# Widening the stationary of the last 64-token tiles from 64 to 128 columns

## The chip, the cores and the metric

The kernel runs on one core of a Trainium2 chip. The metric is the device time of one execution in microseconds (us). Engines are named as the profile does: PE is TensorE's matmuls, PEld its weight loads, DVE is VectorE, ACT is ScalarE, POOL is GpSimd.

## The reference, cut to what matters

Linear attention with a feature map, followed by a two-layer feed-forward block:

```python
# q, k, v: [8 batches, 8 heads, 576 tokens, 64];  w_phi: [64, 128]
def phi(x):                                   # 64 -> 128 -> 256 features
    proj = einsum('bhsd,df->bhsf', x, w_phi)
    proj = proj - max(abs(proj), axis=-1)
    return concatenate([exp(proj), exp(-proj)], axis=-1)
kv  = einsum('bhsf,bhsd->bhfd', phi(k), v)
z   = sum(phi(k), over tokens)
num = einsum('bhsf,bhfd->bhsd', phi(q), kv)
den = einsum('bhsf,bhf->bhs', phi(q), z) + 1e-6
x   = (num / den) as [4608 tokens, 512]
out = relu(x @ w_in)**2 @ w_out               # 512 -> 2048 -> 512
```

Per batch, 576 tokens are four tiles of 128 tokens and one of 64. The change concerns the product that gives num and den for that last tile.

## The kernel before

A list scheduler in Python orders all work in one program. It interleaves the attention of batch b with the feed-forward matmuls (128x512, the bulk of the work) of earlier tokens. Three kinds of TensorE matmul matter. The profile writes the stationary as rows\*columns, "128\*64" being 128 rows by 64 columns:

- feed-forward: 128\*128, mostly 512 moving columns;
- projections of q and k, and the kv product: 64\*128, issued in pairs on rows 0 to 63 and 64 to 127 of their operands (called row-tiled here; in the trace the second of such a pair mostly starts 3 or 4 ns after the first);
- num/den: the stationary is exp(±proj) of one head for the tile's tokens, the moving operand is kv with 65 columns. For a 128-token tile that is 128\*128, for the 64-token tile 128\*64 (called column-tiled here).

The forms that are neither, 128\*128, are called the full array. A switch of mode is a change from one of these three kinds to another. The words sort the forms that the profile lists; what TensorE does at a switch no trace shows, only when things start.

```python
for i, (g0, j0, nj) in enumerate(order_j):          # nj = 2: 128 tokens; nj = 1: 64 tokens
    lo, hi_ = g0 % 2 * 64, (g0 % 2 + nj) * 64       # the tile's rows: 0:128, 0:64 or 64:128
    ...
    # exponentials of the projections, two banks bk, two signs, into qph (t), packed
    nc.scalar.activation(
        out=t.t.rearrange("f pr hi p -> f (pr hi p)")[:, : nj * 512].rearrange(
            "f (r b c) -> f b r c", r=2, b=2)[:, bk],
        in_=w[bk].t[:, : nj * 256].rearrange("f (r c) -> f r c", r=2),
        func=ACT.Exp, scale=sg)
    ...
    for r in range(2):                              # two groups of four heads, a PSUM bank each
        def nd(c, w=w, lo=lo, hi_=hi_):
            return w.t.rearrange("t (h c) -> t h c", h=4)[lo:hi_, :, c]
        def fn(s, ...):                             # s: the sign; four matmuls, one per head
            for z in range(4):
                h = 4 * r + z
                nc.tensor.matmul(
                    out=nd(slice(0, D + 1))[:, z],
                    lhsT=qg[s].t.rearrange("f pr hi p -> f (pr hi p)")[
                        :, h * (hi_ - lo) : (h + 1) * (hi_ - lo)],
                    rhs=kv[r][0].t[:, z % 2, z // 2, s, :],
                    start=(s == 0 and z == 0), stop=True, skip_group_check=True)
        # PE: fn(0); DVE: scale by em; PE: fn(1); DVE: reciprocal of den, then num * that -> xo
    # xo is transposed into xT by DMA (batch 0: by PE); the feed-forward matmuls read xT
```

The eight 64-token tiles issue 8 x 2 x 2 groups of 4, so 128 column-tiled matmuls, out of 4194.

Of the kernel before, what the change touches and what calls it, by code (L numbers as in the profile page):

```python
# [157 lines left out]
def kernel(  # L158
# [12 lines left out]
    B, H, S, D = q.shape  # L171
    Fd = w_phi.shape[1]
    DM, DF = moe_w_in.shape
    P = 128
# [56 lines left out]
    def pe(key, cost, fn, deps=(), bufs=(), rows=128):  # L231
        o = pl.op("pe", cost, key, fn, deps, bufs, lat=350, rows=rows)
        att.append(o)
        return o

    def act(key, n, fn, deps=(), bufs=()):
        return pl.op("act", 60 + 0.83 * n, key, fn, deps, bufs, lat=220 + MARGIN)

    def dve(key, n, fn, deps=(), bufs=()):

        return pl.op("dve", 65 + 1.04 * n, key, fn, deps, bufs, lat=190 + MARGIN)
# [6 lines left out]
    def banks(n):  # L248

        w = [Buf(r_one) for _ in range(n)]  # L250
        for x in w:
            x.token = Buf(r_att)
        return w
# [25 lines left out]
    def begin():  # L279
# [5 lines left out]
        out=scrap[:, 4:8], in_=scrap[:, 0:4], func=ACT.Exp), [o_begin])  # L285
# [56 lines left out]
    def attention(b, x, key):  # L342
# [4 lines left out]
        def transposes(xb, ld, xt, at):  # L347

            ops = []
            if b >= NPE or b and at:  # L350
                for u0, n in GRP:
                    def fn(u0=u0, n=n):
                        nc.sync.dma_start_transpose(
                            out=xt.t[:, u0 // 2 : (u0 + n) // 2, :],
                            in_=xb.t[:, u0 : u0 + n, :].rearrange("x u d -> x (u d)"),
                        )
                    ops.append(xbar(key(at), n * 16, fn, ld[0] + (x["v"][1][0] if b > 1 else []), [xb, xt]))
                return ops
            for u0, n in ((0, 16), (16, 16), (32, 4)) if b or at else GRP:
                w, = banks(1)  # L360

                def fn(u0=u0, n=n, w=w):
                    for i in range(n // 2):
                        nc.tensor.transpose(
                            out=tp(w)[:, i], in_=xb.t[:, u0 + 2 * i : u0 + 2 * i + 2, :]
                            .rearrange("x u d -> x (u d)"), identity=ident)
                kk = key(1 + u0 + 4 * at)
                p_ = pe(kk, 40 + n * 30, fn,
                        [o_id] + ld[0] + (ld[-1] if u0 + n > U // 2 else []), [w, xb, xt])
                ms = slice(u0 // 2, (u0 + n) // 2)  # L370
                if b or at:
                    o = dve(kk, n * 38, lambda w=w, n=n, ms=ms: nc.vector.tensor_copy(
                        out=xt.t[:, ms, :], in_=tp(w)[:, : n // 2]), [p_], [w, xt])
                else:
                    o = act(kk, n * 64, lambda w=w, n=n, ms=ms: nc.scalar.activation(
                        out=xt.t[:, ms, :], in_=tp(w)[:, : n // 2], func=ACT.Copy),
                        [p_], [w, xt])
                ops += [o] * (1 if not (b or at) else (n + 7) // 8)
# [5 lines left out]
        if b:  # L384
            d = pl.op("x", 1000, key(2), None, tq)
            gates[b] = pool(key(2), 100, lambda: nc.gpsimd.tensor_copy(
                out=gate, in_=qT.t[:1, M - 1, P - 8 :]), [d], [qT])
# [4 lines left out]
        if b:  # L392
            def fn():
                nc.gpsimd.memset(va[0].t[:, :, D], 1.0)
                nc.gpsimd.tensor_copy(out=va[0].t[:, :, :D], in_=xv.t)
            o_va = [[pool(key(32), 2400, fn, lv[0] + lv[-1], va[:1] + [xv])] * NG] * 2
# [4 lines left out]
        for g, (u0, n) in enumerate(GRP):  # L401
            kk = key(2 + 8 * g)
            w = banks(2)
            c = n * 64
# [71 lines left out]
        while g0 < (b + 1) * NJ:  # L476
            j0 = jord[b % 2][g0 - b * NJ]
            nj = 1 if j0 == NJ - 1 else 2
# [4 lines left out]
        for hf in range(2):  # L483
            t = Buf(r_kv)
            w = banks(2)

            def kvp(w, hi):
                return w[hi].t.rearrange("f (i c) -> f i c", i=4)[:, :, : D + 1]
            ops = []
            for prl in range(2):  # L490
                pr = 2 * hf + prl
# [18 lines left out]
            for hi in range(2):  # L510
                kk = key(KV_AT[1] + 8 * hf + 6 if b else 20)
                if b or hi:
                    o.append(act(kk, 260, lambda w=w, t=t, hi=hi: nc.scalar.activation(
                        out=t.t[:, hi].rearrange("f pr s c -> f (pr s) c"),
                        in_=kvp(w, hi), func=ACT.Copy), ops, w + [t]))
                else:
                    o.append(dve(kk, 260, lambda w=w, t=t, hi=hi: nc.vector.tensor_copy(
                        out=t.t[:, hi].rearrange("f pr s c -> f (pr s) c"),
                        in_=kvp(w, hi)), ops, w + [t]))
# [5 lines left out]
        for i, (g0, j0, nj) in enumerate(order_j):  # L525
            lo, hi_ = g0 % 2 * 64, (g0 % 2 + nj) * 64
            kk = key(Q2_AT[b > 0][i])
            w, qg = banks(2), [Buf(r_qph), Buf(r_qph)]
# [15 lines left out]
            qe = []  # L544
            for bk in range(2):
                for t, sg in zip(qg, (1.0, -1.0)):
                    def fn(w=w, t=t, sg=sg, nj=nj, bk=bk):
                        nc.scalar.activation(  # L548
                            out=t.t.rearrange("f pr hi p -> f (pr hi p)")[:, : nj * 512].rearrange(
                                "f (r b c) -> f b r c", r=2, b=2)[:, bk],  # L550
                            in_=w[bk].t[:, : nj * 256].rearrange("f (r c) -> f r c", r=2),
                            func=ACT.Exp, scale=sg)
                    qe.append(act(kk, nj * 256, fn, [p_], [w[bk], t]))

# [2 lines left out]
            w, m0, mq, em = banks(2), Buf(r_m0), Buf(r_mq), Buf(r_em)  # L557

            def fn(w=w, j0=j0, nj=nj):
# [12 lines left out]
                out=m0.t[:, bk, : 2 * nj],  # L572
                in_=w[bk].t[:, : nj * 256].rearrange("x (i f) -> x i f", f=Fd),
# [23 lines left out]
            c, tt = tile_of[n2]  # L597
# [8 lines left out]
            for r in range(2):  # L606
                w, = banks(1)
                hs = slice(4 * r, 4 * r + 4)

                def nd(c, w=w, lo=lo, hi_=hi_):  # L610
                    return w.t.rearrange("t (h c) -> t h c", h=4)[lo:hi_, :, c]

                def fn(s, nd=nd, qg=qg, lo=lo, hi_=hi_, r=r):
                    for z in range(4):
                        h = 4 * r + z
                        nc.tensor.matmul(  # L616
                            out=nd(slice(0, D + 1))[:, z],
                            lhsT=qg[s].t.rearrange("f pr hi p -> f (pr hi p)")[
                                :, h * (hi_ - lo) : (h + 1) * (hi_ - lo)],
                            rhs=kv[r][0].t[:, z % 2, z // 2, s, :],  # L620
                            start=(s == 0 and z == 0), stop=True, skip_group_check=True)
                bs = [w, rd, xo, kv[r][0]]
                p_ = pe(kk, 132, lambda fn=fn: fn(0), [o_em] + qe + kv[r][1], bs + [qg[0]])

                def sc(nd=nd, em=em, lo=lo, hi_=hi_, hs=hs):
                    x = nd(slice(0, D + 1))
                    nc.vector.tensor_tensor(  # L627
                        out=x, in0=x, in1=em.t[lo:hi_, hs].to_broadcast(list(x.shape)),
                        op=ALU.mult)
                dk = kk - 20  # L630
                d_ = dve(dk, 260, sc, [p_, o_em], [w, em])
                p_ = pe(dk, 132, lambda fn=fn: fn(1), [d_], bs + [qg[1]])
                d_ = dve(dk, 50, lambda nd=nd, rd=rd, lo=lo, hi_=hi_, hs=hs:
                    nc.vector.reciprocal(out=rd.t[lo:hi_, hs], in_=nd(D)), [p_], [w, rd])

                def fn(nd=nd, rd=rd, xo=xo, lo=lo, hi_=hi_, hs=hs):
                    x = nd(slice(0, D))
                    nc.vector.tensor_tensor(  # L638
                        out=xo.t[lo:hi_].rearrange("t (h d) -> t h d", h=H)[:, hs],
                        in0=x, in1=rd.t[lo:hi_, hs].to_broadcast(list(x.shape)), op=ALU.mult)  # L640
                parts.append(dve(dk, 250, fn, [d_], [w, rd, xo]))
            nds.append(p_)
            if hi_ == P and b == 0:
                w, = banks(1)
# [159 lines left out]
```

## Time and profile before

| | before |
|---|---|
| median of 3 runs (range) | 383.3 us (382.87 to 383.75) |
| span of the profiled execution | 382.5 us |
| PE busy | 366.7 us, 96% |
| DVE / ACT / POOL busy | 65% / 64% / 49% |

Lines of the page of the kernel before: the span, the busy time of the engines, and the chain of work that ended last, by engine and by line. L708 and L679 are the two feed-forward products, L616 is num/den, L500 is the kv product. Of the names in these lines, win and wout are w_in and w_out, qph and kph are phi(q) and phi(k), mk and ksh are the largest absolute value of a k projection and the projection less it, va is v with an added column that gives z, xo is num / den and xT its transpose, hr is the relu and h its square; "one" is any PSUM bank, PSUM being the memory that TensorE writes to.

```profile
span 382.5 us, 10585 instructions
...
PE 366.7 (96%) x4194; PEld 200.9 (53%) x4194; DVE 247.7 (65%) x554; ACT 244.4 (64%) x485; POOL 185.9 (49%) x317
...
PE 74%; DMA 11%; DVE 9%; issue 3%; POOL 1%; DVEq 0%; POOLq 0%
```

PE is three quarters of the chain. The DMA part is loading in the first 49 us (of w_out 8%, of v 2%), and the DVE part is a few stretches in which PE waits for VectorE. A busy share alone would not say that a saved nanosecond counts; the chain says that it does, outside those stretches. (The durations do not give the cost of a matmul: in this trace a 128x512 matmul is recorded with 380 ns, yet the next starts 216 ns after it. So all costs below are read from starts, not from durations.)

Groups by form of the kernel before (line, engine, operation, operands, stationary, shapes, count; busy us, mean ns of one; idle before):

```profile
L616 PE MATMUL one<-kv_sb,qph 128*128 128x65 bf16 x512 | 28.5, 195 | 1.5 <-DVE one L627 1.4
L616 PE MATMUL one<-kv_sb,qph 128*64 128x65 bf16 x128 | 9.1, 200 | 0.0
...
L616 PEld LDWEIGHTS <-qph 128*128 128x128 bf16 x512 | 23.6, 98 | 13.6 <-issue 2.9
L616 PEld LDWEIGHTS <-qph 128*64 128x64 bf16 x128 | 6.1, 110 | 8.6 <-issue 8.5
```

The mean durations of the two forms hardly differ (195 and 200 ns). What the 128\*64 form costs is seen in when things start.

Over the whole trace, matmul by matmul: 309 ns from a 512-column matmul into a 128\*64 run (otherwise 216), and 128 ns out of it (otherwise 30).

### The profile page before, as it was taken

The numbers are of one execution on the slowest core, as the hardware profiler recorded it, in microseconds if no ns is written. First come the engines' busy times: TensorE is split into PE (matmuls) and PEld (weight loads), VectorE is DVE, ScalarE is ACT, GpSimd is POOL, SyncE is SP. The second block draws the span as 40 slices with busy tenths as digits, with TensorE's granted clock in tenths as the row PEclk, the third lists the DMA queues.
The fourth block names the chain that finished last, engine by engine and source line by source line (L and its number), as shares of the span: only waits on it lengthen the run. The fifth ranks groups of instructions, "written<-read, shape, count | busy, mean of one in ns | idle before, by whom it ended". The sixth has DMA issues, their size and how long they took to land.

```text
span 382.5 us, 10585 instructions
## 1 busy us (share of the span) xinstructions
PE 366.7 (96%) x4194; PEld 200.9 (53%) x4194; DVE 247.7 (65%) x554; ACT 244.4 (64%) x485; POOL 185.9 (49%) x317
## 2 busy tenths in 40 slices
PE   8989999978999999999999999999999999999994
PEld 8868857544544454545543544455446444444442
DVE  1857894899279738973699488956895843333221
ACT  3785788649972986489758974996399733333300
POOL 8533766507890986079728674677446420000000
PEclk9998999999999999999999999999999999999998
DMA  7999994257944595459665946495631422112123
GB/s 114 213 208 205 162 174 73 48 91 133 195 50 89 91 217 62 80 105 202 99 85 109 169 85 104 91 196 102 105 77 30 71 55 49 35 29 55 27 64 75
DMA packets 70721, 40.41 MB, mean 106 GB/s; under 512 B 51088, under 2 KB 65552, under 8 KB 70672
## 3 DMA queue, kind: packets, MB, share of 16 engines
q1 hardware_dynamic: 55360, 21.38, 31.2%
q0 software_dynamic: 15312, 18.35, 29.4%
q8 instruction: 33, 0.54, 0.6%
q14 instruction: 16, 0.13, 0.1%
HBM read 36.77 MB, written 9.44 MB: 121 GB/s over the span
## 4 chain that ended last, share of the span: by engine, by line
PE 74%; DMA 11%; DVE 9%; issue 3%; POOL 1%; DVEq 0%; POOLq 0%
PE one L708 32%; PE one L679 25%; DMA wout<-in_moe_w_out_dram 8%; PE one L616 5%; PE one L500 5%; DVE mk L423 4%; DVE ksh L433 3%; PE one L538 3%; DMA xv<-in_v_dram 2%; PE one L567 2%; PE one L412 2%; DVE ot L715 1%; DVE xo L638 1%; POOL va L467 1%; DVE one L627 1%
## 5 line engine op out<-in xcount | busy, mean ns | idle before, releaser
L687 POOL TENSOR_TENSOR h<-hr 128x512 bf16<-128x512 bf16 x112 | 115.2, 1042 | 83.7 <-ACT hr L684 81.7
L679 PE MATMUL one<-xT,win 128*128 128x512 bf16 (+2 forms) x704 | 144.2, 341 | 2.8 <-DVE ksh L433 2.8
L708 PE MATMUL one<-wout,h 128*128 128x512 bf16 x576 | 144.5, 380 | 0.8 <-DMA wout<-in_moe_w_out_dram 0.5
L684 ACT ACTIVATE hr<-one 128x512 bf16<-128x512 f32 x144 | 84.5, 603 | 67.7 <-PE one L679 59.8
L548 ACT ACTIVATE qph<-one 128x512 bf16<-128x512 f32 (+1 forms) x160 | 77.9, 563 | 19.5 <-PE one L538 19.3
L679 PEld LDWEIGHTS <-win 128*128 128x128 bf16 x704 | 59.2, 98 | 54.6 <-issue 3.5
L708 PEld LDWEIGHTS <-h 128*128 128x128 bf16 x576 | 51.0, 98 | 56.6 <-issue 1.4
L441 ACT ACTIVATE kph<-ksh 128x1024 bf16<-128x1024 f32 (+1 forms) x70 | 64.8, 964 | 19.7 <-DVE ksh L433 19.2
L571 DVE TENSOR_REDUCE m<-one 128x4 f32<-128x512 f32 (+1 forms) x80 | 47.9, 630 | 41.7 <-PE one L567 24.9
L423 DVE TENSOR_REDUCE mk<-one 128x4 f32<-128x512 f32 (+1 forms) x80 | 49.7, 627 | 8.3 <-PE one L412 8.2
L433 DVE TENSOR_TENSOR ksh<-one,mk 128x512 f32<-128x512 f32 (+1 forms) x70 | 44.7, 638 | 3.8
L715 DVE COPY ot<-one 128x512 f32<-128x512 f32 x36 | 24.7, 685 | 28.2 <-PE one L708 28.0
L580 POOL COPY mq<-m 64x4 f32<-64x4 f32 x144 | 26.5, 184 | 32.0 <-DVE m L571 27.3
L616 PEld LDWEIGHTS <-qph 128*128 128x128 bf16 (+1 forms) x640 | 29.7, 100 | 22.2 <-issue 11.3
L616 PE MATMUL one<-kv_sb,qph 128*128 128x65 bf16 (+1 forms) x640 | 36.9, 196 | 1.5 <-DVE one L627 1.4
L627 DVE TENSOR_TENSOR one<-one,em 128x260 f32<-128x260 f32 (+1 forms) x80 | 31.5, 429 | 5.8 <-PE one L616 2.3
L638 DVE TENSOR_TENSOR xo<-one,rden 128x256 bf16<-128x256 f32 (+1 forms) x80 | 31.7, 419 | 0.8
L690 DVE TENSOR_TENSOR h<-hr 128x512 bf16<-128x512 bf16 x32 | 13.5, 423 | 24.4 <-ACT hr L684 24.4
L323 PE MATMUL one<-ones 128*128 128x128 bf16 x316 | 24.0, 236 | 1.1 <-DVE scrap L281 1.1
L500 PE MATMUL one<-va,kph 64*128 64x65 bf16 x1152 | 22.8, 191 | 0.9 <-issue 0.9
L500 PEld LDWEIGHTS <-kph 64*128 64x128 bf16 x1152 | 20.5, 94 | 4.3 <-issue 3.3
L323 PEld LDWEIGHTS <-ones 128*128 128x128 bf16 x316 | 20.6, 106 | 2.5 <-DVE scrap L281 1.1
(43 smaller groups left out, 184.5 us busy)
## 6 DMA issues: line engine op xcount, KB each, us to landing
out_dram<-ot SPq DMA_DIRECT2D x72, 128.0 KB, 2.4
xk<-in_k_dram POOLq DMA_DIRECT2D x7, 576.0 KB, 6.1
xq<-in_q_dram POOLq DMA_DIRECT2D x7, 576.0 KB, 9.8
xv<-in_v_dram POOLq DMA_DIRECT2D x7, 576.0 KB, 12.2
win<-in_moe_w_in_dram POOLq DMA_DIRECT2D x1, 2048.0 KB, 18.5
wout<-in_moe_w_out_dram POOLq DMA_DIRECT2D x1, 2048.0 KB, 32.4
xk<-in_k_dram POOLq DMA_DIRECT2D x2, 288.0 KB, 5.6
xq<-in_q_dram POOLq DMA_DIRECT2D x2, 288.0 KB, 7.6
```

The lines of the kernel that those rows point to most:

```text
L323: nc.tensor.matmul(out=r_one.tiles[7][:, :P], lhsT=ones, rhs=ones, start=True, stop=True)
L423: nc.vector.tensor_reduce(out=mk.t[:, e, ms], in_=wv(e), axis=AX.X, op=ALU.max, apply_absolute_value=True)
L433: nc.vector.tensor_tensor(out=ksh.t[:, e, : n // 2, :], in0=wv(e), in1=mk.t[:, e, ms].to_broadcast([P, n // 2, Fd]), op=ALU.subtract)
L441: nc.scalar.activation(out=t.t[:, :, : n // 2, :].rearrange("x e i f -> x e (i f)"), in_=ksh.t[:, :, : n // 2, :].rearrange("x e i f -> x ...
L500: nc.tensor.matmul(out=kvp(w, hi)[:, 2 * prl + s], lhsT=kph[g][s].t[r, i % 2, i // 2, :], rhs=va[s].t[r, u, : D + 1], start=(j == 0), stop ...
L548: nc.scalar.activation(out=t.t.rearrange("f pr hi p -> f (pr hi p)")[:, : nj * 512].rearrange("f (r b c) -> f b r c", r=2, b=2)[:, bk], in ...
L571: d1 = [dve(kk, nj * 256, lambda w=w, m0=m0, nj=nj, bk=bk: nc.vector.tensor_reduce(out=m0.t[:, bk, : 2 * nj], in_=w[bk].t[:, : nj * 256].r ...
L616: nc.tensor.matmul(out=nd(slice(0, D + 1))[:, z], lhsT=qg[s].t.rearrange("f pr hi p -> f (pr hi p)")[:, h * (hi_ - lo) : (h + 1) * (hi_ - ...
L679: nc.tensor.matmul(out=w.t[:, y * n : (y + 1) * n], lhsT=win[:, kc, mc * P : (mc + 1) * P], rhs=xT.t[:, a:z, kc, :], start=(kc == 0), stop ...
L684: o = act(key - 4, TCH, lambda: nc.scalar.activation(out=r.t, in_=w.t, func=ACT.Relu), [p_], [w, r])
L687: o = pool(key - 4, 1050, lambda: nc.gpsimd.tensor_tensor(out=t.t, in0=r.t, in1=r.t, op=ALU.mult), [o], [r, t])
L708: nc.tensor.matmul(out=w.t, lhsT=h2[c, mc, tt][0].t[:, h2[c, mc, tt][1] :][:, :P], rhs=wout[:, mc, :], start=(mc == 0), stop=(mc == KC2 - 1))
```

## The change

The intent: give the 64-token tile a 128-column stationary too, so that no matmul has the column-tiled form. The exponentials of the 64 tokens are written into their half (lo:hi_) of a full 128-wide slot; the other half keeps what an earlier tile left there. The product then gives 128 rows, of which 64 are garbage that nobody reads. Core of the diff:

```diff
-    out=t.t.rearrange("f pr hi p -> f (pr hi p)")[:, : nj * 512].rearrange(
-        "f (r b c) -> f b r c", r=2, b=2)[:, bk],
-    in_=w[bk].t[:, : nj * 256].rearrange("f (r c) -> f r c", r=2),
+    out=t.t.rearrange("f (r b) hi p -> f b r hi p", b=2)[:, bk, :, :, lo:hi_],
+    in_=w[bk].t[:, : nj * 256].rearrange(
+        "f (r hi c) -> f r hi c", r=2, hi=2),
...
-    out=nd(slice(0, D + 1))[:, z],
-    lhsT=qg[s].t.rearrange("f pr hi p -> f (pr hi p)")[
-        :, h * (hi_ - lo) : (h + 1) * (hi_ - lo)],
+    out=w.t[:, z * P : z * P + D + 1],
+    lhsT=qg[s].t[:, h // 2, h % 2, :],
```

The order of instructions on every engine stays the same.

More of the change, by code (lines that the diff above doesn't have):

```diff
@@ L546, in attention, with fn @@
                 for t, sg in zip(qg, (1.0, -1.0)):
-                    def fn(w=w, t=t, sg=sg, nj=nj, bk=bk):
+                    def fn(w=w, t=t, sg=sg, nj=nj, bk=bk, lo=lo, hi_=hi_):
                         nc.scalar.activation(
-                            out=t.t.rearrange("f pr hi p -> f (pr hi p)")[:, : nj * 512].rearrange(
-                                "f (r b c) -> f b r c", r=2, b=2)[:, bk],
-                            in_=w[bk].t[:, : nj * 256].rearrange("f (r c) -> f r c", r=2),
+                            out=t.t.rearrange("f (r b) hi p -> f b r hi p", b=2)[:, bk, :, :, lo:hi_],
+                            in_=w[bk].t[:, : nj * 256].rearrange(
+                                "f (r hi c) -> f r hi c", r=2, hi=2),
                             func=ACT.Exp, scale=sg)
@@ L611, in nd, with fn @@
                     return w.t.rearrange("t (h c) -> t h c", h=4)[lo:hi_, :, c]
-                def fn(s, nd=nd, qg=qg, lo=lo, hi_=hi_, r=r):
+                def fn(s, w=w, qg=qg, r=r):
                     for z in range(4):
```

## The prediction

> **What bounds the kernel now.** TensorE. The page shows PE busy 366.7 of a 382.5 us span (96%) at full clock; after the first 49 us, which wait for weights from DMA, the chain of waits is PE matmuls almost throughout. Exceptions are four stretches that hang on VectorE's mk/ksh work (about 78 to 92, 126 to 134, 169 to 174, 195 to 209 us). PE time saved outside them should shorten the program one for one.
>
> **What the change removes.** The 64-token tiles issue 128 matmuls in the form 128\*64 (by-form groups), in 27 unbroken runs of 4 or 8. From matmul starts in the timeline, one to the next:
>
> - Into such a run from a 128\*128 matmul of 512 columns: 309 ns, where that matmul is otherwise followed after 216 ns. Excess 93 ns (93 to 95 ns after 256 or 65 columns). 23 of 27 entries are of this kind.
> - Out of such a run into a 128\*128 matmul: 127 to 129 ns, against 30 ns out of a 128\*128 matmul of 65 columns. Excess 97 ns, 24 of 27 exits.
> - Inside a run: 3.8 us over 101 steps, some 37 ns each, against 30 ns in the 128\*128 form: 0.7 us in all.
>
> The other entries and exits neighbour 64\*128 matmuls (row-tiled projections), where a switch remains: 200 ns from 64\*128 to 128\*64, 201 ns to 128\*128. No gain.
>
> [...] the trace's weight loads take 110 ns for 128x64 column-tiled and 98 ns for 128x128, so twice the columns should cost nothing.
>
> Sum: 23 x 93 + 24 x 97 + 700 ns = 5.2 us of PE time (1.4%).
>
> **What it adds or moves.** No instruction is added and the order is the same on all engines; only forms differ. The matmuls now write all 128 PSUM partitions, half of them garbage nobody reads; streaming is still 65 columns, so it costs no time. The exponentials of those tiles (32 of 128x256, 393 ns each) write runs of 64 instead of 128 elements; I expect no visible change, and ACT (64% busy) is off the chain.
>
> **How much is on the critical path.** Four runs (197 to 201 us) lie where VectorE, full from 195 to 209 us, ends the wait: their 0.7 us should be swallowed. The others precede a PE-timed point: after the first seven (52 to 70 us), VectorE idles for PE at 69 to 70 us and starts from PE again at 78.5 us, so it moves forward too. That leaves about 4.5 us.
>
> **Prediction: 378.8 us (383.3 - 4.5), range 377.4 to 380.9.** Faster by over 2%: 3%; within 2%: 95%; slower by over 2%: 2%. A real gain, of 1.2%.
>
> **What the profile would show.**
> 1. No 128\*64 form; all 640 kv_sb x qph matmuls in one form.
> 2. Entries at 216 ns, exits and inner steps at 30 ns; these tiles' weight loads at 98 ns.
> 3. ACT exponentials of 128x256 still near 393 ns.
> 4. The FFN tail after 310 us unchanged in length, starting about 4.5 us earlier.
> 5. VectorE-bound stretches keep their length; PE's wait at 207 to 209 us grows by some 0.7 us.
>
> **What would make it wrong.** If a full-width load of these weights can't be hidden, entries shrink less. If the earlier PE meets more VectorE or DMA waits, down to 2 us could remain. If PE and VectorE fall into better step, a little more than 5 us is possible, but 2% (7.7 us) exceeds all PE time removed.

The 5.2 us (less 0.7, about 4.5) come from the starts in the trace of before. So does the remark that streaming 65 columns into 128 partitions costs no time: in that trace the next matmul of the full array starts 30 ns after a 128\*128 matmul of 65 moving columns, 56 ns after one of 128, 109 ns after one of 256 and 216 ns after one of 512 (medians).

## More of the kernel before

All runs of one kernel in one job lie within 1% of each other (the widest 382.10 to 385.49 us); all runs quoted here were classed fast, at a granted TensorE clock of 0.99 to 1.00. In each job the kernel before ran beside the tested one on the same chip; the three jobs of experiments ran on three chips, so kernels of two jobs are best compared by their ratio to the kernel before.

From the timeline of the kernel before (start us, us, engine, line, operation, operands, form, count):

```profile
52.96 1.04 PE L708 MATMUL one<-wout,h 128*128 128x512 bf16 x4
53.93 0.31 PE L616 MATMUL one<-kv_sb,qph 128*64 128x65 bf16 x4
54.17 0.50 PE L679 MATMUL one<-xT,win 128*128 128x256 bf16 x3
```

Four 512-column matmuls take 4 x 216 = 864 ns when more of their kind follow. Here the column-tiled run starts 970 ns after the first of them, and it holds PE for 240 ns, where four steps of 30 ns would be 120.

The weight loads at this place show what kind of cost it is; first before, then the kernel after (where L707 is the old L708):

```profile
53.40 0.10 PEld L708 LDWEIGHTS <-h 128*128 128x128 bf16 x1
53.92 0.20 PEld L616 LDWEIGHTS <-qph 128*64 128x64 bf16 x4 [0.42 <-issue]
...
52.25 0.10 PEld L707 LDWEIGHTS <-h 128*128 128x128 bf16 x1
52.47 0.38 PEld L616 LDWEIGHTS <-qph 128*128 128x128 bf16 x4
```

After, the first load of the run starts 2 ns after the last 512-column matmul has started, and so beside it. Before, it starts only 307 ns after that matmul, and its own matmul 2 ns after it. At all 15 entries from a 512-column matmul that the trace of before shows without a wait, the load starts 306 to 308 ns after that matmul; after, 1 or 2 ns. So at a switch the load starts late as well as the matmul; the excess of 93 ns passes before the load starts, so it is not the duration of a slow load.

## The result, and the profile after

| | before | after |
|---|---|---|
| first job, median of 4 runs (range) | 383.52 us (382.87 to 384.66) | 380.22 us (378.70 to 380.45) |
| ratio (95% interval) | | 0.9901 (0.9876 to 0.9925) |
| repeat in another job, median | 383.43 us (11 runs) | 378.68 us (4 runs), ratio 0.9882 |
| span of the profiled execution | 382.5 us | 378.7 us |
| PE busy | 366.7 us | 362.4 us |

A ratio here is the mean time of one kernel's fast runs over that of the other's of the same rounds, so it is not quite the ratio of the medians. The gain is about 1%, inside the predicted range of 377.4 to 380.9 us. The predicted middle, 378.8 us, lies between the two jobs' medians.

The page after (source lines below the changed product stand one line higher: L707 is the old L708, L678 the old L679):

```profile
span 378.7 us, 10586 instructions
...
PE 362.4 (96%) x4194; PEld 201.3 (53%) x4194; DVE 247.0 (65%) x554; ACT 244.1 (64%) x485; POOL 185.8 (49%) x317
...
PE 81%; DVE 13%; issue 3%; DMA 1%; ACT 1%; DVEq 0%; ACTq 0%
```

The chain's DMA share fell from 11% to 1%, but not because of the change. In the trace of before, the first matmul on wout waited for its load; in this trace the load came just early enough. In the repeats below it is the other way around, 2% before and 10% after. The shares of a chain can swing like that on the half microsecond that PE waited for wout.

Groups by form after:

```profile
L616 PE MATMUL one<-kv_sb,qph 128*128 128x65 bf16 x640 | 35.2, 194 | 1.6 <-DVE one L626 1.4
...
L616 PEld LDWEIGHTS <-qph 128*128 128x128 bf16 x640 | 29.9, 98 | 18.4 <-issue 4.1
```

There is one form, and the weight loads take 98 ns. The timeline at the same place in the program:

```profile
51.82 1.03 PE L707 MATMUL one<-wout,h 128*128 128x512 bf16 x4
52.68 0.28 PE L616 MATMUL one<-kv_sb,qph 128*128 128x65 bf16 x4
52.80 0.60 PE L678 MATMUL one<-xT,win 128*128 128x256 bf16 x4
```

The run now starts 860 ns after the four feed-forward matmuls began (970 before) and holds PE for 120 ns (240 before). This one run saves 0.23 us.

### A ledger of the time

Both traces record all 4194 matmuls in the same order, so each matmul's start after can be taken from its start before. I call the difference the lead, and note where it changes:

| place (time before) | change of the lead, us |
|---|---|
| start: first matmul on wout, at 49.5 us | +0.94 |
| at the 128\*64 runs outside 195 to 211 us | +4.26 |
| at and between the 4 runs within 195 to 211 us | +0.00 |
| 56 us, a wait for VectorE | -0.29 |
| 162 us, a wait for DMA-transposed xT | -0.60 |
| 183 us, a standstill in the kv product | -0.67 |
| the rest | +0.21 |
| sum, at the last matmul | +3.85 |

So outside 195 to 211 us the change delivered at the runs nearly what was costed (4.26 of 4.5 us). Parts were lost elsewhere, and something unrelated was won at the start. The waits of PE, from the waits view (engine, line, what it waited for: us in total, times, longest), before:

```profile
PE one L679 <- DVE ksh L433: 2.8, 5, 0.7
...
PE one L500 <- issue: 0.9, 1, 0.9
...
PE one L708 <- DMA wout<-in_moe_w_out_dram: 0.5, 1, 0.5
```

and after:

```profile
PE one L678 <- DVE ksh L433: 2.8, 5, 0.7
...
PE one L500 <- issue: 1.5, 1, 1.5
...
PE one L678 <- DMA xT<-xo: 0.4, 1, 0.4
...
PE one L678 <- ACT hr L683: 0.3, 1, 0.3
```

The old waits for VectorE are unchanged. Waits for xT and for ACT's hr are new, and the wait called "issue" in the kv product (L500) grew by 0.6 us. "Issue" means that the profile shows nothing that PE waited for.

### The profile page after: what moved, and what is told of

Read it like the earlier page. It is cut to its first block, busy times and chain, and to the rows that moved or that the text cites. A ratio compares the mean times of both kernels' runs of the same rounds, so it can differ in the third digit from the quotient of the medians.

```text
span 378.7 us, 10586 instructions
## 1 busy us (share of the span) xinstructions
PE 362.4 (96%) x4194; PEld 201.3 (53%) x4194; DVE 247.0 (65%) x554; ACT 244.1 (64%) x485; POOL 185.8 (49%) x317
## 4 chain that ended last, share of the span: by engine, by line
PE 81%; DVE 13%; issue 3%; DMA 1%; ACT 1%; DVEq 0%; ACTq 0%
PE one L707 30%; PE one L678 26%; PE one L323 6%; DVE mk L423 5%; PE one L500 5%; PE one L616 5%; DVE ksh L433 4%; PE one L538 3%; PE one L567 3%; PE one L412 2%; DMA xT<-xo 1%; DVE xo L637 1%; DVE one L626 1%; DVE ot L714 1%; PE one L364 1%
## 5 line engine op out<-in xcount | busy, mean ns | idle before, releaser
L678 PE MATMUL one<-xT,win 128*128 128x512 bf16 (+2 forms) x704 | 144.0, 340 | 3.7 <-DVE ksh L433 2.8
L707 PE MATMUL one<-wout,h 128*128 128x512 bf16 x576 | 144.3, 379 | 0.3 <-DVE ksh L433 0.3
L678 PEld LDWEIGHTS <-win 128*128 128x128 bf16 x704 | 59.4, 98 | 55.5 <-issue 4.2
L707 PEld LDWEIGHTS <-h 128*128 128x128 bf16 x576 | 51.1, 98 | 55.7 <-issue 1.4
L423 DVE TENSOR_REDUCE mk<-one 128x4 f32<-128x512 f32 (+1 forms) x80 | 49.7, 627 | 8.9 <-PE one L412 8.8
L616 PEld LDWEIGHTS <-qph 128*128 128x128 bf16 x640 | 29.9, 98 | 18.4 <-issue 4.1
L616 PE MATMUL one<-kv_sb,qph 128*128 128x65 bf16 x640 | 35.2, 194 | 1.6 <-DVE one L626 1.4
L323 PE MATMUL one<-ones 128*128 128x128 bf16 x316 | 24.8, 241 | 1.1 <-DVE scrap L281 1.1
L500 PE MATMUL one<-va,kph 64*128 64x65 bf16 x1152 | 22.7, 190 | 1.5 <-issue 1.5
L500 PEld LDWEIGHTS <-kph 64*128 64x128 bf16 x1152 | 20.5, 94 | 4.9 <-issue 4.0
L323 PEld LDWEIGHTS <-ones 128*128 128x128 bf16 x316 | 21.5, 110 | 2.6 <-DVE scrap L281 1.1
```

Of the source, the lines that this page charges most:

```text
L323: nc.tensor.matmul(out=r_one.tiles[7][:, :P], lhsT=ones, rhs=ones, start=True, stop=True)
L423: nc.vector.tensor_reduce(out=mk.t[:, e, ms], in_=wv(e), axis=AX.X, op=ALU.max, apply_absolute_value=True)
L500: nc.tensor.matmul(out=kvp(w, hi)[:, 2 * prl + s], lhsT=kph[g][s].t[r, i % 2, i // 2, :], rhs=va[s].t[r, u, : D + 1], start=(j == 0), stop ...
L616: nc.tensor.matmul(out=w.t[:, z * P : z * P + D + 1], lhsT=qg[s].t[:, h // 2, h % 2, :], rhs=kv[r][0].t[:, z % 2, z // 2, s, :], start=(s ...
L678: nc.tensor.matmul(out=w.t[:, y * n : (y + 1) * n], lhsT=win[:, kc, mc * P : (mc + 1) * P], rhs=xT.t[:, a:z, kc, :], start=(kc == 0), stop ...
L707: nc.tensor.matmul(out=w.t, lhsT=h2[c, mc, tt][0].t[:, h2[c, mc, tt][1] :][:, :P], rhs=wout[:, mc, :], start=(mc == 0), stop=(mc == KC2 - 1))
```

## The experiments

All outputs are right. "Lead from 52 to 310 us" below is my working from the traces: the start of the same ACT instruction in the trace of before less that in the run's trace, at 310 us less the same at 52 us. It leaves the start out. ACT is used because some traces lack up to 1% of the matmul records, while all of these kernels record the same number of ACT instructions (two kernels with moved copies are compared with each other). The point at 52 us (L653, 51.96 us) matters: from the next ACT instruction, at 52.45 us, some leads come out up to 0.31 us higher (first trace of after +3.30, the null +0.34, half the dose +1.98). Differences of 0.3 us between leads say nothing.

### Is it chance? Both kernels again

No edit.

> The changed kernel once more, unedited. Every theory: about 0.990 of the kernel before (0.987 to 0.993). What its trace is for: aligned matmul by matmul with the first trace of before, the lead of the changed kernel grew by about 0.22 us at each of the 27 runs of 64-token matmuls, but four things moved it otherwise: +0.94 us at 49 us (the weights wout landed earlier), -0.58 us at 159 us (wait for the DMA-transposed xT), -0.68 us at 181 us (a gap inside the kv matmuls just after a 16 KB instruction fetch), -0.7 us at 197 to 205 us (VectorE). Systematic consequences of the change must come back in this trace: I expect the waits at 159 and at 197 to 205 us to do so within 0.2 us; chance effects of DMA must not: I expect the start (wout) and the instruction-fetch gap to be different by several tenths of a us.

> The kernel before once more, unedited: the null of the method. Ratio 1.000, within 0.997 to 1.003. Its trace must show the same entries (309 ns) and exits (128 ns) of the 128*64 runs. If the start differs from the first trace of before by several tenths of a us, the 0.94 us lead that the changed kernel had at 49 us is chance and not the change.

| | median | ratio (95%) | lead from 52 to 310 us | first matmul on wout |
|---|---|---|---|---|
| first trace of after | 380.22 | 0.9901 (0.9876 to 0.9925) | +2.99 | 48.55 us |
| after again | 378.68 | 0.9882 (0.9866 to 0.9899) | +3.76 | 47.43 us |
| before again | 383.65 | 1.0005 (0.9991 to 1.0019) | +0.03 | 49.21 us |

The null is a null. In the repeat of the changed kernel the waits at 195 to 199 us came back to within 3 ns (excess over the usual step 448 and 311 ns, first 451 and 309), so they belong to the change; all six traces without a column-tiled matmul, relief aside, have the wait for hr there, 0.26 to 0.29 us idle. The wait for xT came back too, but with 0.33 instead of 0.60 us, a wider spread than I expected. In two further traces (65 columns and half the dose) it is 0.53 and 0.54 us, but in three of the changed kernel (with dummies, and with more warm-up matmuls) it is not there at all: the step is 33 or 34 ns. It is thus no fixed price of the change, and what decides it is not shown. The wait at 56 us did not come back. The start differed by 1.1 us between two traces of the same kernel. Over all traces it lies between 48.0 and 49.7 us in the kernels that stay column-tiled and between 47.4 and 49.1 us in the others, and up to there the two programs do the same; I take it for chance of the loads. It makes up 1.1 of the 2.0 us between the profiled spans of the changed kernel (378.7 and 376.7 us), so a time difference of one microsecond between two kernels is not to be read as theirs.

### Theory and rivals for the gain

Theory A: each switch of mode costs PE time, about 95 ns on the way in and 97 ns on the way out. Rival B: the form itself is slow, above all its weight loads (110 against 98 ns). Rival C: the other layout of qph did it.

**The new layout, but column-tiled** (against the changed kernel):

```diff
-    out=w.t[:, z * P : z * P + D + 1],
-    lhsT=qg[s].t[:, h // 2, h % 2, :],
+    out=w.t[lo:hi_, z * P : z * P + D + 1],
+    lhsT=qg[s].t[:, h // 2, h % 2, lo:hi_],
```

> The changed kernel with its new place of the exponentials in qph, but multiplied again with a 64-column stationary into 64 PSUM partitions. Theory A (the gain is the avoided switch of tiling mode): as the kernel before, ratio 1.000 (0.997 to 1.003), with entries of 309 ns and exits of 128 ns. Rival C (the gain is the other layout: the exponential's writes, or the stationary's reads): as the changed kernel, ratio 0.990.

Measured: 383.76 us, ratio 1.0012 (0.9996 to 1.0028), lead -0.18 us, entries 309 ns, exits 128 ns. Rival C is out: the layout gives nothing.

**65 columns in half of the groups** (against the changed kernel; n is 65 where the tile lies in the lower half, else 128):

```diff
-    out=w.t[:, z * P : z * P + D + 1],
-    lhsT=qg[s].t[:, h // 2, h % 2, :],
+    out=w.t[:n, z * P : z * P + D + 1],
+    lhsT=qg[s].t[:, h // 2, h % 2, :n],
```

> The changed kernel, but the 16 groups of the batches whose 64-token tile lies in the lower half use 65 stationary columns instead of 128 (the result stays right). [...] Theory A (the mode switch costs the time): keeps the whole gain, ratio 0.990 (0.987 to 0.993); entries 216 ns, exits 30 ns, no form 128*64. Rival B (the gain is that a 128-column weight load is faster, 98 against 110 ns, and hidden): loses the gain of these 16 of 32 groups, ratio about 0.995, and their weight loads take over 98 ns with entries or steps longer than those of the 128-column groups.

That 128\*65 counts as the full array, which theory A needs here, was the assumption; the starts below test it.

Measured: 380.12 us, ratio 0.9921 (0.9898 to 0.9945), lead +3.70 us, as the repeat of the changed kernel has it (+3.76). The weight loads, by form:

```profile
L616 PEld LDWEIGHTS <-qph 128*128 128x128 bf16 x576 | 26.4, 97 | 15.9 <-issue 3.7
...
L616 PEld LDWEIGHTS <-qph 128*65 128x65 bf16 x64 | 4.1, 114 | 2.4 <-issue 0.4
```

and the timeline of this run at the place shown before:

```profile
51.90 1.03 PE L707 MATMUL one<-wout,h 128*128 128x512 bf16 x4
52.76 0.29 PE L616 MATMUL one<-kv_sb,qph 128*65 128x65 bf16 x4
52.90 1.03 PE L678 MATMUL one<-xT,win 128*128 128x256 bf16 x8
```

The loads of 65 columns are the slowest of all (114 ns), and yet the run starts 860 ns after its predecessors began and lasts 140 ns instead of 240: entries are 216 ns and exits 36 ns. Here the load of 114 ns delays no entry, while the form 128\*64 with its load of 110 ns has entries of 309 ns: it is the switch that costs, not the slow load. The ratio alone is not sharp enough to say this (its interval just excludes the 0.995 of rival B); the starts are.

**Half the dose** (n is 64 instead of 65 in the edit above):

> Half the dose: only the 64-token tiles of the upper half (16 of the 32 groups of 4) use 128 stationary columns; those of the lower half stay column-tiled. Theory A (a cost for each switch of mode): about half of the gain, ratio 0.995 (0.992 to 0.998); the remaining 128*64 runs keep entries of 309 ns and exits of 128 ns. If the gain were a better phase between the engines rather than a sum of small costs, the half would give either nothing (1.000) or all (0.990).

Measured: 381.52 us, ratio 0.9943 (0.9919 to 0.9968), lead +1.67 us; the 13 runs that are left keep entries of 309 ns and exits of 128 ns. About half, as a sum of small costs should give.

**More switches, same matmuls.** In the kernel before, and as a control in the changed one, a dummy matmul after the second of each four:

```diff
     start=(s == 0 and z == 0), stop=True, skip_group_check=True)
+    if nj == 1 and z == 1:
+        nc.tensor.matmul(out=w.t[:, P - 8 : P], lhsT=ident, rhs=wphi2[:, :8],
+                         start=False, stop=True, skip_group_check=True)
```

> The kernel before, with one dummy full-array matmul of 8 columns (into PSUM columns that nobody reads) after the second of each four 128*64 matmuls: the same 128 column-tiled matmuls, but one more exit and one more entry in each of 32 groups. Theory A: each costs as the existing ones do, an exit of 128 ns and an entry of about 122 ns in place of one step of 37 ns, so 32 x 213 ns = 6.8 us of PE time, of which some 0.9 us lies where VectorE ends the wait (195 to 209 us): +5 to +6.5 us, ratio 1.013 to 1.017. Rival B (the form itself is slow, each matmul or each weight load): the dummies cost only their own 30 ns, about 1 us, ratio 1.0025.

> The control for the run before: the same 32 dummy matmuls in the changed kernel, where they switch nothing. Every theory: their own 30 ns each, about +0.9 us over the changed kernel, ratio to before about 0.9915 (0.988 to 0.995). The difference to the run with dummies in the kernel before is then 9 to 10.5 us under theory A, against 4 us under rival B.

Measured: in the kernel before 388.05 us, ratio 1.012 (1.0093 to 1.0146), lead -5.38 us; in the changed kernel 378.66 us, ratio 0.987 (0.9844 to 0.9895), lead +4.70 us. The timeline of the first:

```profile
51.68 1.04 PE L712 MATMUL one<-wout,h 128*128 128x512 bf16 x4
52.65 0.25 PE L616 MATMUL one<-kv_sb,qph 128*64 128x65 bf16 x2
52.83 0.18 PE L623 MATMUL one<-wphi,ident 128*128 128x8 bf16 x1
52.94 0.25 PE L616 MATMUL one<-kv_sb,qph 128*64 128x65 bf16 x2
53.12 1.05 PE L683 MATMUL one<-xT,win 128*128 128x256 bf16 x8
```

The dummy starts 130 ns after the matmul before it (32 times, 127 to 132 ns), and the column-tiled form starts again 109 ns after the dummy. The two medians differ by 9.4 us, inside the 9 to 10.5 us of theory A and far from the 4 us of rival B. But each ran 1 to 2 us faster than I had expected; both ratios missed. A likely reason is in the traces: the standstill of 1 us in the kv product, which every run before had, was in neither. (The run with dummies in the changed kernel also lacks the wait for xT.) This led to the next pair.

### The standstill in the kv product

From the timelines, at the same matmuls of the program, before:

```profile
182.38 0.22 PE L500 MATMUL one<-va,kph 64*128 64x65 bf16 x3
183.46 0.62 PE L500 MATMUL one<-va,kph 64*128 64x65 bf16 x28 [0.86 <-issue]
```

and after:

```profile
179.70 0.22 PE L500 MATMUL one<-va,kph 64*128 64x65 bf16 x3
181.45 0.69 PE L500 MATMUL one<-va,kph 64*128 64x65 bf16 x33 [1.53 <-issue]
```

PE stops between the third and the fourth of 18 matmuls of one scheduled group, where the program has no wait. The page lists a DMA queue of kind instruction (kernel before):

```profile
q8 instruction: 33, 0.54, 0.6%
```

These are 33 packets of 16,384 bytes. PE has 8388 matmuls and weight loads, so if this queue feeds PE, a packet holds some 254 of them, by estimate. In all seven traces that have the standstill at this place, one such packet started 1.0 to 1.4 us before PE stopped, and PE went on 1.24 to 1.57 us after it had landed. The kv matmuls start every 16 ns on average, two instructions each (a load and a matmul). So theory F: PE ran out of instructions. If the packets hold PE's instructions in their order, more warm-up matmuls at the very start make each packet begin at an earlier place of the program. The edit does that:

```diff
     def warm():
+        if not warmed:
+            warmed.append(1)
+            for _ in range(64):                      # 16 in the second run
+                nc.tensor.matmul(out=r_one.tiles[7][:, :8], lhsT=ones, rhs=ones[:, :8],
+                                 start=True, stop=True)
         for _ in range(2):
```

> The changed kernel with 64 more warm-up matmuls of 8 columns at the very start (128 more PE instructions, while PE waits for data anyway)[...]. In every trace so far PE stands still for 1.2 to 1.7 us inside the kv matmuls at about 181 us, with no wait in the program there, and goes on 1.24 to 1.57 us after a 16 KB instruction packet landed. Theory F (PE had run out of instructions): the gap at this matmul vanishes or shrinks by over 0.5 us (another may open elsewhere), and the time is 0 to 1.3 us below the changed kernel. Rival S (it waits for data of another engine): the gap stays at the same matmul, 1.0 to 1.7 us long. The start may be later by up to 1 us, as it is by chance too.

> The changed kernel with 16 instead of 64 more warm-up matmuls (32 PE instructions). With 128 more instructions the gap at 181 us vanished and one of 1.0 us opened in an earlier batch's kv matmuls; the two runs with dummies, which had some 32 more instructions by then, had no such gap anywhere. Theory F: no gap of over 0.5 us within kv matmuls, and the time is 1.0 to 1.5 us below the changed kernel: ratio to before 0.986 to 0.988. If the place did not matter, 0.990 with the gap at 181 us.

Measured with 64: 378.28 us, ratio 0.9866 (0.984 to 0.9893). The standstill is gone from its old place and a new one stands in an earlier batch's kv product; the timeline of this run, first the old place, then the new one (L507 is the old L500):

```profile
179.42 0.73 PE L507 MATMUL one<-va,kph 64*128 64x65 bf16 x36
...
138.91 0.29 PE L507 MATMUL one<-va,kph 64*128 64x65 bf16 x8
140.18 0.61 PE L507 MATMUL one<-va,kph 64*128 64x65 bf16 x28 [0.99 <-issue]
```

Again a packet landed before PE went on, 1.5 us earlier. Measured with 16: 379.32 us, ratio 0.9907 (0.9888 to 0.9926). At 181 us there is no standstill, and the largest within kv matmuls after the start is one of 0.32 us at 250 us; the lead is +4.60 us, 0.8 us more than in the repeat of the changed kernel. The time does not show it and misses the expectation: this run's start was late (first matmul on wout at 49.03 us, against 47.43 us in the repeat). The expectation of no gap over 0.5 us missed too: a kv product at 27.35 us, before the start, has one of 1.95 us.

Counting settles more than the times do. I count two instructions for each weight load that has started. At the old place PE stops after 4796 instructions in all seven traces. The counts are written here in blocks of 256, the largest step that fits them (two of those below are 960 and 1216, just 256 apart) and close to the 254 per packet estimated above: 4796 is 18 x 256 + 188. With 64 more warm-up matmuls it stops after 4032 (15 x 256 + 192), with 16 more after 960 (3 x 256 + 192) and 6588 (25 x 256 + 188). All lie within four instructions of the same place in a block of 256. In the other traces too PE stops near 27 us after 960 instructions, for 1.7 to 2.3 us; only the run with 64 more has this stop later, after 1216 (4 x 256 + 192) and for 1.12 us. The profile puts the stop after 960 down to ScalarE's qph. But with 16 more it comes after the same count at another matmul, with no wait, and with 64 more the matmuls that qph seemed to hold run through. However the stream is moved, the stops keep their place in a block of 256 and change their matmul. So they hang on the count of instructions, as theory F has it, and a wait for data is out for the standstill in the kv product. How PE gets its instructions is not shown beyond that. The times do not test it: the two ratios (0.9866 and 0.9907) lie on both sides of the changed kernel's own (0.9882 and 0.9901), with intervals that overlap. Whether 16 more warm-up matmuls are worth their place by the clock stays open at this spread.

The standstill is there in both kernels. That it was 0.67 us longer in the first trace after than before is chance as far as these runs show: over the traces the idle time is 0.86, 0.86 and 1.14 us in the kernels that stay column-tiled throughout, and 1.53, 1.27, 1.27 and 1.04 us in those with the change or a part of it. A small systematic part can't be excluded.

### Where VectorE swallows the gain

In 195 to 209 us (windows of the kernel before) VectorE is busy 13.59 of 14.00 us. PE gets its banks and its inputs from it there, directly or through ScalarE, so PE starts early and then waits. The timeline after, where the loss is taken:

```profile
195.17 1.03 PE L678 MATMUL one<-xT,win 128*128 128x512 bf16 x4
196.03 0.78 PE L616 MATMUL one<-kv_sb,qph 128*128 128x65 bf16 x16
197.10 1.89 PE L678 MATMUL one<-xT,win 128*128 128x512 bf16 x8 [0.29 <-ACT hr L683]
199.13 0.28 PE L616 MATMUL one<-kv_sb,qph 128*128 128x65 bf16 x4
...
195.51 1.06 ACT L441 ACTIVATE kph<-ksh 128x1024 bf16<-128x1024 f32 x1 [2.80 <-DVE ksh L433]
196.47 0.58 ACT L683 ACTIVATE hr<-one 128x512 bf16<-128x512 f32 x1
```

The matmul at 197.10 is released by ScalarE's hr, but that hr stood behind a kph for which ScalarE had waited 2.80 us for VectorE's ksh.

Theory V says that this is where, with the DMA-transposed xT that hangs on VectorE's xo, the missing part of the gain went. To test it, both kernels got less work on VectorE:

```diff
-    d = dve(key - 2, 560, lambda: nc.vector.tensor_copy(out=o.t, in_=w.t), [p_], [w, out_, o])
+    if c < DVE_FROM:                                 # the first 7 of 9 chunks
+        d = act(key - 2, 560, lambda: nc.scalar.activation(
+            out=o.t, in_=w.t, func=ACT.Copy), [p_], [w, out_, o])
+    else:
+        d = dve(key - 2, 560, lambda: nc.vector.tensor_copy(out=o.t, in_=w.t), [p_], [w, out_, o])
```

> The kernel before, with the 28 copies of a finished output tile (512 columns, 0.68 us each) of the first seven chunks moved from VectorE to ScalarE; the scheduler then places everything anew. It is the base for the next run. By itself: fewer waits for VectorE in the four VectorE-bound stretches, more work for ScalarE; I expect ratio 0.985 to 1.005.

> The changed kernel with the same 28 copies on ScalarE. Theory V (what the change did not deliver of its 5.2 us was mostly swallowed where VectorE, or the transposing DMA behind it, ends the wait): with VectorE relieved the gain between this run and the relieved kernel before is 4.6 to 5.4 us, where the two original kernels differ by about 3.9 us. Rival W (the PE time removed was over-estimated, or is swallowed elsewhere): the two relieved kernels differ by 3.9 us or less. A gap of over 1 us from an instruction fetch in one of the two and not in the other would have to be taken out of the comparison.

Measured: relieved before 382.18 us, ratio 0.997 (0.9951 to 0.999); relieved after 377.46 us, ratio 0.9852 (0.9827 to 0.9877). The medians differ by 4.7 us, and by starts the lead from 52 to 310 us is +4.32 us. The scheduler now makes 25 runs of the 128\*64 matmuls, with 21 entries and 20 exits that neighbour the full form; by the same costs (93 and 98 ns, and 0.7 us for the steps inside) that is an estimate of 4.6 us. So 94% arrived, against 2.99 to 3.76 of 5.2 us in the originals. Matmul by matmul, the lead grows by 4.42 us at the 25 runs. Elsewhere it rises by 1.4 us between 80 and 90 us and falls back by as much before 100 us, and falls once for good, by 0.24 us at 141 us; nothing is lost near 160 us or near 200 us. This supports theory V. It doesn't settle it by itself: the scheduler has moved the runs themselves, the new order also happens to have no standstill of this kind after 30 us, the wait for xT is missing in three unrelieved traces too, and by time alone 4.7 us is not to be told from the 4.75 us between the medians of the repeat.

The relieved changed kernel has the lowest median and the lowest ratio to before (0.9852). The interval of that ratio overlaps those of the changed kernel in some jobs, so that it is faster than the changed kernel is not shown; that it is faster than the kernel before is.

## Why the prediction was right

1. **The bound.** Right, but not one for one all the way. At the runs outside 195 to 211 us +4.26 us was won, where about 4.5 us had been put down; of this, 0.29 and 0.60 us were lost again in the first trace in front of waits at 56 and 162 us (point 7).
2. **The cost per switch.** Right: 93 ns in and 97 ns out were removed; entries are 216 ns and exits 29 to 34 ns afterwards. The experiments show that it is the switch: the cost follows the number of switches (half the dose: lead +1.67 us; more switches: -5.38 us), not the layout (-0.18 us) and not the weight loads (+3.70 us with loads of 114 ns).
3. **Twice the columns cost nothing.** Right: 98 ns per load, 29 to 30 ns per step.
4. **ScalarE's exponentials.** Right: 392 ns after, 393 before, for the 32 of 128x256.
5. **The tail.** The part after 310 us starts 3.85 us earlier in the first trace where 4.5 us was predicted, and its length did not change. Of the 3.85 us, 0.94 are the early start, which is not the change's doing.
6. **The four swallowed runs.** Right in size (about 0.7 us predicted, all of it gained nothing), wrong in place: the waits at 207 to 209 us did not grow (0.61 and 0.30 us idle in both traces). The time was lost at the runs themselves, in front of the matmuls at 197 and 199 us.
7. **What was left out.** The prediction had four stretches bound by VectorE and checked only them. A fifth point, the wait for xT at 160 us, had little or no slack: in the repeat of the kernel before, the step there was 66 ns longer than usual, with no idle time recorded, so a PE that comes earlier may have to wait. It took 0.60 us in the first trace and 0.33 in the repeat, and nothing in three later traces. The prediction named DMA waits among what could go wrong and allowed for a gain of only 2 us, but it did not name this point. It also did not know of the standstill in the kv product, which took 0.67 us of the first trace, nor of a start that moves by a microsecond, which gave 0.94 us back. The last two nearly cancel. So it is partly luck that the result is as near to the predicted number as it is; that the switches cost the time, and how much at the runs, is not luck.

## What to carry to other kernels

On a PE-bound kernel, count the switches of mode rather than the matmuls of each form. (128\*65 beside 128\*128 is another form too, and its entries stayed at 216 ns. A switch into the row-tiled form costs as much as one into the column-tiled: 312 ns from a 512-column matmul into a projection, where 216 is usual.) A short run of small matmuls in the column-tiled form cost here some 190 ns beside its work (93 ns on the way in, 97 on the way out), more than the four matmuls themselves, and padding the stationary with garbage columns that nobody reads was free here. Read such costs from the distance between starts, since the durations of the two forms differed by 5 ns only. And before counting on a saving, look for the points that PE reaches with no slack: a wait that isn't in the profile because it is just zero can swallow a gain as a long one does. PE can also stand still in a dense stretch with no wait in the program: here in kv products, with matmuls every 16 ns, for 0.32 to 1.95 us, always 188 or 192 instructions past a multiple of 256, at matmuls that moved when instructions were added earlier in the program.
